# A long convolution and a switch layer on one core: the convolution in another stated order, its last round through the PSUM banks by halves

## The chip, the cores and the metric

The kernel runs on one core of a Trainium2 chip, written with Bass and Tile. The metric is the device time of one execution in microseconds. Before the change it is 543.25 us (median of three executions, 541.98 to 543.84). All rows below come from one further execution, recorded by the hardware profiler.

## The reference

A layer of an H3 model with 2048 tokens of 512 channels, followed by a mixture of 8 experts of which each token takes one.

```python
h  = x + q' * (conv(kv) + kv * ssm_D)        # q' = layernorm(x); x is A_q
#   kv = (4-tap causal convolution of A_k with shift_k) * A_v
#   conv(kv): causal convolution over all 2048 tokens with ssm_k,
#             channel by channel, in the reference by an FFT of length 4096
hn = layernorm(h)
e  = argmax(hn @ w_gate)                     # one expert per token
out = h + silu(hn @ w1[e]) @ w2[e]           # the gate of a single expert is 1
```

The means and variances of both layer norms go over the 512 channels of a token. All is in fp32.

## The kernel before

The program has three parts that follow one another: the convolution stage, in which `h` and the router's logits are made (until about 182 us), the routing (until about 196 us), and the experts (until the end). The change is in the first part; in the other two only a few small tables get another place in memory, and their instructions keep their order.

**The convolution stage.** The 512 channels are worked through in four blocks of 128 (`c` = 0 to 3), the 2048 tokens in four units of 512 (`u` = 0 to 3). The long convolution is a transform in two steps with a product between. For a block, the kernel does this, and each line names the engine:

- `first_tap` and `tap` (ScalarE, `L255`, `L263`), `add_tap` (GpSimd, `L267`) and, for the first block, `taps` (VectorE, `L272`) make the short convolution of A_k from the buffer `kt`, of which there is one. `turn_kv` (TensorE, `L279`) transposes it, `times_v` (VectorE, `L282`) multiplies by A_v.
- `stage_a` (TensorE, `L295`) is the transform's first step, once for the signal (`u`) and once for the channel's kernel (`k`), 16 times a block, through two PSUM buffers `pa`; `keep_a` (ScalarE, `L298`) brings each to SBUF.
- Then the block is taken in two halves of its channels, so that there are eight **rounds** `i` = 0 to 7. A round is a chain: `turn` for `u` and for `k` (VectorE, `L320`, 32x32 transposes into `xa` and `xb`); `stage_b("u")` (TensorE, `L331`, 16 matmuls of 32x32x512 over four banks of PSUM, the buffer `pb`); `keep_u` (ScalarE, `L337`, the four banks to SBUF); `stage_b("k1")`; `product1` (VectorE, `L340`); `stage_b("k2")`; `product2` (VectorE, `L344`); `back` (TensorE, `L331`, 32 matmuls: the way back); `unturn` (VectorE, `L352`).
- `pb` is one buffer of four banks. Each of the steps `stage_b`, `stage_b`, `stage_b`, `back` writes all of it anew, and so waits until the step before has been read.
- `last_stage` (TensorE, `L367`, through `pa`), `gate` (VectorE, `L371`), `residual` (GpSimd `L374`, on VectorE in the last block), `store_h`, `stats` (VectorE, `L381`, for the second layer norm), `turn_kv` of `h`, `keep_h` (ScalarE, `L384`), `logits` (TensorE, `L402`) and `sum_logits` (VectorE, `L411`) finish a block, unit by unit. `stats1` (VectorE, `L419`, `L420`) and `norm_x` (GpSimd, `L360`) are the first layer norm. `aggr` (VectorE, `L415`) closes the second. `stay_warm` (`L394`) issues matmuls without use at the end of the stage.

While a round's chain waits for another engine, an engine does the next block's first steps or the last block's last ones. The routing starts with `L646` (TensorE) and `L651` (VectorE), after the last `sum_logits` and `aggr`.

**What sets the order.** The steps are not written in the order of their issue. Each `add(...)` gives a step with its engine, an estimated cost, a due time, what it uses and what it makes; `Plan.run` then goes through them greedily and issues, engine by engine, the step that can start first and is due first. The tile framework sees the order of issue and puts the semaphores in. Every buffer (`BUF`, `PBUF`) is a ring of so many places; a place that is used again waits for the readers of what it held. Loads go through SyncE (SP) in the order of issue, and a load waits for the one eight places before it in its queue.

Of the kernel before, what the change touches and what calls it, by code (L numbers as in the profile page):

```python
# [11 lines left out]
I32 = mybir.dt.int32  # L12
# [19 lines left out]
for _n, _w in (("id", 128), ("b", 128), ("m", 128), ("tri", 128), ("one", 128),  # L32
               ("iota", 128), ("tile", 24), ("e", 8), ("key", 8), ("ta", 1), ("tb", 16),
               ("si", 64), ("ei", 64), ("cap", 8), ("tight", 64), ("ft", 128), ("scan", 128)):
    COLS[_n] = (C_N, C_N + _w)
    C_N += _w


class Plan:
# [33 lines left out]
    def run(self, pace, zero, ahead, latency=0.08, load=2.5, slack=0.25):  # L73
        ring = {b: [] for b in self.bufs}
        done, free, n_left = {}, {}, len(self.steps)
        need = [len(s[5]) for s in self.steps]
        then = [[] for _ in self.steps]
        for n, s in enumerate(self.steps):
            for m in s[5]:
                then[m].append(n)  # L80
        ready = {n for n, k in enumerate(need) if not k}
        moved = 0.0

        def start(n):
            eng, cost, due, fn, args, after, turn = self.steps[n]
            t = max(free.get(eng, 0.0), zero + pace * (due - ahead))
            wait = set(after)
            for b, k, place in turn:
                if place is not None and place != len(ring[b]):
                    return None  # L90
                if len(ring[b]) >= self.bufs[b]:
                    old = ring[b][-self.bufs[b]]
                    wait |= set(self.writers[old]) | set(self.readers[old])
            for m in wait:
                if m not in done:
                    return None
                e = self.steps[m][0]
                t = max(t, done[m] + (0.0 if e == eng else load if e == "SP" else latency))
            return t

        while n_left:
            best = {}
            for n in ready:
                t = start(n)
                if t is not None:
                    best.setdefault(self.steps[n][0], []).append((t, self.steps[n][2], n))
            assert best, [self.steps[n][3:5] for n in sorted(ready)[:9]]
            picks = []
            for c in best.values():
# [1113 lines left out]
```

## Time and profile before

| | us |
|---|---|
| median of three executions (541.98 to 543.84) | 543.25 |
| the profiled execution: its own time | 543.93 |
| the profiled execution: span from first to last instruction | 542.0 |
| convolution stage, to the first routing step of VectorE | 182.21 |
| the last round, from its first `stage_b` to the first `last_stage` behind it | 15.70 |
| from there to the first routing step of VectorE | 13.32 |

The profiled execution's time exceeds its span by 1.9 us and the median by 0.68 us. A row of a timeline has the start, the duration, the engine, the line, the operation with the tiles written and read, and the number of instructions that it groups; in square brackets stands how long the engine had been idle before, and which instruction of another engine ended that. The table of stretches shows which engine is full in a stretch: a busy time close to the stretch's length.

### The profile page before, as it was taken

How to read it: one execution, taken by the hardware profiler on the slowest of the kernel's cores; microseconds unless marked ns; L12 is line 12 of the kernel's file. 1: busy time of each engine (PE TensorE's matmuls, PEld its weight loads, DVE VectorE, ACT ScalarE, POOL GpSimd, SP SyncE). 2: the span in 40 equal slices, each digit the busy share in tenths (PEclk: the TensorE clock that was granted, in tenths of full speed). 3: DMA queues.
4: the chain of work that ended last, by engine and by line, in shares of the span. 5: the costliest groups of instructions: out<-in, count | busy, mean ns of one | idle time of the engine just before them, and what ended most of it. 6: DMA issues, size and time to landing. Idle time of an engine off the chain costs nothing.

```text
span 542.0 us, 12326 instructions
## 1 busy us (share of the span) xinstructions
PE 521.0 (96%) x4875; PEld 455.3 (84%) x4875; DVE 391.8 (72%) x556; ACT 264.6 (49%) x410; POOL 279.1 (52%) x324
## 2 busy tenths in 40 slices
PE   8999989999998989999999999999999999999994
PEld 8967777767656879689999999999988988988973
DVE  3779899898997979679655775864856765765851
ACT  2787887534321346545435444555544644554520
POOL 0455649865653237828703841850870850851832
PEclk9999999999999999999999999999999999999998
DMA  8919686659651378675554565665658557666401
GB/s 280 393 47 282 224 276 187 191 144 303 182 159 52 95 241 302 199 271 179 172 195 145 194 186 186 202 207 183 200 171 285 182 174 264 199 189 232 155 2 39
DMA packets 41156, 105.26 MB, mean 194 GB/s; under 512 B 5174, under 2 KB 13496, under 8 KB 40706
## 3 DMA queue, kind: packets, MB, share of 16 engines
q1 hardware_dynamic: 37682, 95.89, 53.9%
q0 software_dynamic: 3408, 8.51, 4.8%
q8 instruction: 40, 0.66, 0.5%
q14 instruction: 26, 0.21, 0.1%
HBM read 95.96 MB, written 8.50 MB: 193 GB/s over the span
## 4 chain that ended last, share of the span: by engine, by line
PE 80%; DVE 6%; issue 4%; DMA 4%; ACT 3%; POOL 1%; SPq 1%; POOLq 0%; DVEq 0%
PE acc L900 30%; PE acc L921 15%; PE acc L924 12%; PE pa L295 8%; PE pb L331 7%; PE pa L367 5%; DMA kt<-in_kt_dram 3%; PE pm L279 2%; PE pt L855 1%; DVE xa L344 1%; DVE zs L352 1%; DMA kt<-h_dram,idx 1%; PE pt L944 1%; DVE bst L381 1%; ACT ac L263 1%
## 5 line engine op out<-in xcount | busy, mean ns | idle before, releaser
L882 DVE TENSOR_TENSOR wlo<-raw,whi 128x1024 fp32r<-128x1024 f32 (+1 forms) x113 | 155.4, 1385 | 36.3 <-ACT whi L877 36.1
L905 POOL TENSOR_TENSOR hl<-s,hh 128x240 fp32r<-128x240 f32 (+5 forms) x112 | 102.8, 935 | 135.9 <-DVE hh L904 135.3
L877 ACT ACTIVATE whi<-raw 128x1024 fp32r<-128x1024 f32 x112 | 114.6, 1052 | 7.4 <-DMA raw<-in_w_dram 3.1
L903 ACT ACTIVATE s<-acc 128x240 f32<-128x240 f32 (+5 forms) x112 | 43.1, 387 | 113.0 <-PE acc L900 62.2
L904 DVE CAST hh<-s 128x240 fp32r<-128x240 f32 (+5 forms) x112 | 47.3, 430 | 54.4 <-ACT s L903 54.2
L900 PE MATMUL acc<-xh,whi 128*128 128x240 f32 (+5 forms) x448 | 72.6, 285 | 0.2 <-ACT xh L856 0.2
L900 PE MATMUL acc<-xl,whi 128*128 128x240 f32 (+5 forms) x448 | 71.8, 283 | 0.0
L900 PE MATMUL acc<-xh,wlo 128*128 128x240 f32 (+5 forms) x448 | 71.8, 283 | 0.0
L900 PEld LDWEIGHTS acc<-xh,whi 128*128 128x128 f32 x448 | 61.6, 189 | 0.9 <-ACT xh L856 0.4
L900 PEld LDWEIGHTS acc<-xl,whi 128*128 128x128 f32 x448 | 61.4, 189 | 0.0
L900 PEld LDWEIGHTS acc<-xh,wlo 128*128 128x128 f32 x448 | 61.3, 189 | 0.0
L921 PE MATMUL acc<-whi,hh 128*128 128x512 f32 (+2 forms) x136 | 54.4, 400 | 0.0
L921 PE MATMUL acc<-whi,hl 128*128 128x512 f32 (+2 forms) x136 | 53.7, 395 | 0.0
L921 PE MATMUL acc<-wlo,hh 128*128 128x512 f32 (+2 forms) x136 | 53.4, 393 | 0.0
L267 POOL TENSOR_TENSOR acc<-acc,ac 128x512 f32<-128x512 f32 x26 | 33.1, 1282 | 36.7 <-ACT acc L255 18.3
L924 PE MATMUL acc<-hh,whi 128*128 128x304 f32 (+2 forms) x168 | 49.7, 296 | 0.0
L924 PE MATMUL acc<-hl,whi 128*128 128x304 f32 (+2 forms) x168 | 49.2, 293 | 0.0
L924 PE MATMUL acc<-hh,wlo 128*128 128x304 f32 (+2 forms) x168 | 49.2, 293 | 0.0
L298 ACT ACTIVATE st<-pa 128x512 f32<-128x512 f32 x64 | 37.3, 595 | 19.6 <-PE pa L295 19.2
L295 PEld LDWEIGHTS pa<-kv,tw 128*128 128x128 f32 x256 | 30.2, 191 | 12.2 <-ACT st L298 8.7
L295 PE MATMUL pa<-kv,tw 128*128 128x128 f32 x256 | 33.5, 282 | 2.2 <-ACT st L298 2.2
L924 PEld LDWEIGHTS acc<-hh,whi 128*128 128x128 f32 x168 | 31.6, 188 | 0.1
(196 smaller groups left out, 892.4 us busy)
## 6 DMA issues: line engine op xcount, KB each, us to landing
raw<-in_w_dram SPq DMA_DIRECT2D x112, 512.0 KB, 4.2
tv<-in_tab_v_dram SPq DMA_DIRECT2D x12, 512.0 KB, 4.3
h<-in_q_dram SPq DMA_DIRECT2D x16, 256.0 KB, 5.1
kt<-in_kt_dram SPq DMA_DIRECT2D x3, 1216.0 KB, 8.0
v<-in_v_dram SPq DMA_DIRECT2D x12, 256.0 KB, 4.4
kern<-in_ssm_dram SPq DMA_DIRECT2D x12, 256.0 KB, 3.7
h<-in_x_dram SPq DMA_DIRECT2D x12, 256.0 KB, 3.5
h_dram<-h SPq DMA_DIRECT2D x12, 256.0 KB, 4.1
```

The lines of the kernel that those rows point to most:

```text
L267: nc.gpsimd.tensor_add(T[a, c, u], T[a, c, u], T[b, c, u])
L295: nc.tensor.matmul(p[:, :, j], tw[:, u * UJ + j, r, :], src[:, j, :], start=True, stop=True)
L298: nc.scalar.activation(T["s" + kind, c][:, r * NU + u], T["pa", kind, c, u, r], AF.Copy)
L331: nc.tensor.matmul(out[b, g, :], w[a], x[a, g, :], start=n == 0, stop=n == len(parts) - 1)
L877: nc.scalar.activation(whi, RAW[s], AF.Copy)
L882: nc.vector.tensor_sub(wlo[:, a:b], RAW[s][:, a:b], whi[:, a:b].bitcast(F32))
L900: nc.tensor.matmul(pu, a[:, k, at], b[:, k, :], start=i == k == 0, stop=i == 2 and k == ND - 1)
L903: nc.scalar.activation(s, pu, AF.Silu)
L904: nc.vector.tensor_copy(hh[:, f, :], s)
L905: nc.gpsimd.tensor_sub(hl[:, f, :], s, hh[:, f, :].bitcast(F32))
L921: nc.tensor.matmul(pd[:ds_.stop - ds_.start], b[:, f, ds_], a[:, f % 2, :], start=f == 0 and i == 0, stop=f == last - 1 and i == 2)
L924: nc.tensor.matmul(pd, a[:, f % 2, ds_], b[:, f, :], start=f == 0 and i == 0, stop=f == 2 * NCH - 1 and i == 2)
```

## The change

There are four parts.

1. **The order.** `Plan.run` with its costs, due times and pace is gone. A list `STEPS` names the 611 steps (603 before) in the order of their issue, and `run` only asserts that the list is possible. The set of steps is the same but for round 7; the order differs on all five engines throughout the convolution stage.
2. **The last round by halves.** For `i` = 7, `stage_b`, `keep_u`, `product1`, `product2`, `back` and `unturn` come twice, for the columns 0 to 255 and 256 to 511 of each of the four banks. The buffer `pb` is taken once for the whole round (`(buf, "both")`), and its halves are slices of it; `p1` likewise. `stay_warm` uses the same tile.
3. **Buffers.** `h` (rows of x) has four places instead of three, `ht` (the turned rows) three instead of two. The space comes from the constants: `cs` holds 1017 columns instead of 1281 (the load of its larger part is 128x889 instead of 128x1153), and the tables that the routing writes late (`mr0`, `tabs_e` and others) lie in a pool `latep` in the space that the convolution stage has left.
4. **The first loads.** `kt` for the first unit is the first DMA of SyncE (before, a table `tw` of 512 KB came first); the larger part of `cs` is the 15th (before, the 10th).

The core of the diff:

```diff
-    def run(self, pace, zero, ahead, latency=0.08, load=2.5, slack=0.25):
...
+    def run(self, order):
+        assert sorted(order) == list(range(len(self.steps)))
+        ring, made = {b: [] for b in self.bufs}, set()
+        for n in order:
             eng, cost, due, fn, args, after, turn = self.steps[n]
...
-               h=(3, quad), xn=(2, quad), tv=(2, [P, UJ, 2, P]), ht=(2, quad))
+               h=(4, quad), xn=(2, quad), tv=(2, [P, UJ, 2, P]), ht=(3, quad))
...
+    def four(buf, key):
+        make = pt if buf == "pb" else sb
+        if len(key) == 2:
+            return make(buf, key, *([[P, NG, 512]] if buf == "pb" else []))
+        if not taken[buf]:
+            make(buf, (buf, "both"), *([[P, NG, 512]] if buf == "pb" else []))
+        half = len(taken[buf]) % 2
+        taken[buf].append(key)
+        T[key] = T[buf, "both"][:, :, 256 * half:256 * half + 256]
+        return T[key]
...
-    def stage_b(kind, k, i):
-        blocks(pt("pb", ("b" + kind, i), [P, NG, 512]), [(k, by_group(T["t" + kind[0], i]))], False)
+    def stage_b(kind, k, i, *y):
+        blocks(four("pb", ("b" + kind, i, *y)), [(k, by_group(T["t" + kind[0], i], *y))], False)
...
+            for y in range(2):
+                tu, tk = [("tu", i), ("tu", i, y)], [("tk", i)]
+                add("PE", 0.7, 0, stage_b, "u", 0, i, y, uses=[*tu, "cb"], behind=["pb"] if y else [],
+                    makes=([] if y else [("pb", "pb")]) + [("pb2", ("bu", i, y))])
+                add("ACT", 1.0, 0, keep_u, i, y, uses=[("bu", i, y), ("tu", i)], mods=[("tu", i, y)])
+                add("PE", 0.7, 0, stage_b, "k1", 1, i, y, uses=[*tk, "cb"], behind=[("bu", i, y)],
+                    makes=[("pb2", ("bk1", i, y))])
...
+                add("PE", 1.25, 0, back, i, y, uses=[("p1", i, y), *tu, "cb"], makes=[("pb2", ("pz", i, y))])
+                add("DVE", 1.2, 0, unturn, i, y, uses=[("pz", i, y)], puts=[("zs", c)])
...
+    STEPS = """
+    48 1 52 49 0 50 54 74 75 2 55 51 6 76 77 56 53 59 57 80 66 60 82 7 81 65 78 84 83 58 68 91 63 8 79 61 62 85 70
...
-    plan.run(PACE, ZERO, AHEAD)
+    plan.run([int(n) for n in STEPS.split()])
```

What the order of the built program shows at the three places that matter most. In these rows `[waits ...]` names the engines or DMA queues whose semaphores an instruction waits on.

TensorE in the last round, before: the logits of an earlier unit, `stage_b("k2")` for round 7, one `last_stage`, `back`.

```order
L402 MATMUL pm<-ht,wgc 32x128 [waits Activation_49]
L402 MATMUL pm<-ht,wgc 32x128 x7
L331 MATMUL pb<-xa,cb 32x512 [waits DVE_49]
L331 MATMUL pb<-xa,cb 32x512 x15
L367 MATMUL pa<-zs,tv 128x128 [waits DMAHW2_49]
L367 MATMUL pa<-zs,tv 128x128 x7
L331 MATMUL pb<-p_2090,cb 32x512 [waits DVE_49]
L331 MATMUL pb<-p_2090,cb 32x512 x15
L331 MATMUL pb<-xb,cb 32x512 x16
```

TensorE at the same place now: `stage_b("k2")` for the first half, one `last_stage` (`pa<-zs,tv`), `stage_b("k2")` for the second half, `back` for the first and for the second half.

```order
L306 MATMUL pb<-xa,cb 32x256 [waits DVE_49]
L306 MATMUL pb<-xa,cb 32x256 x15
L346 MATMUL pa<-zs,tv 128x128 [waits DMAHW5_49]
L346 MATMUL pa<-zs,tv 128x128 x7
L306 MATMUL pb<-xa,cb 32x256 [waits DVE_49]
L306 MATMUL pb<-xa,cb 32x256 x15
L306 MATMUL pb<-p_2112,cb 32x256 [waits DVE_49]
L306 MATMUL pb<-p_2112,cb 32x256 x15
L306 MATMUL pb<-xb,cb 32x256 x16
L306 MATMUL pb<-p_2112,cb 32x256 [waits DVE_49]
L306 MATMUL pb<-p_2112,cb 32x256 x15
L306 MATMUL pb<-xb,cb 32x256 x16
```

The single steps have become pairs, and each of the five groups begins with a wait for VectorE; the `last_stage` stands between the two halves of `stage_b("k2")`.

VectorE in the last round, before: `product1`, two groups of `stats` with one `sum_logits` between, `product2`, one `gate`, `unturn`, one `sum_logits`.

```order
L340 TENSOR_TENSOR p_2090<-pb,xb 128x2048 [waits PE_49,Activation_49]
L381 BN_STATS bst_64<-h 128x6 [waits Pool_49]
L381 BN_STATS bst_64<-h 128x6 x3
L411 TENSOR_TENSOR lacc<-pm,lacc 128x128 [waits DVE_49,PE_49]
L381 BN_STATS bst_64<-h 128x6 [waits Pool_49]
L381 BN_STATS bst_64<-h 128x6 x3
L344 TENSOR_TENSOR xb<-pb,xb 128x2048 [waits DVE_49,PE_49]
L371 TENSOR_TENSOR xn<-pa,xn 128x512 [waits PE_49,Pool_49]
L352 STREAM_TRANSPOSE zs<-pb 128x64x16x2 [waits PE_49]
L411 TENSOR_TENSOR lacc<-pm,lacc 128x128 [waits DVE_49,PE_49]
```

VectorE there now: the halves of `product1`, a `sum_logits`, the halves of `product2` with a `gate` between, the halves of `unturn`, then `stats`.

```order
L315 TENSOR_TENSOR p_2112<-pb,xb 128x4x256 [waits DVE_49,PE_49,Activation_49]
L315 TENSOR_TENSOR p_2112<-pb,xb 128x4x256 [waits PE_49]
L388 TENSOR_TENSOR lacc<-pm,lacc 128x128 [waits DVE_49]
L319 TENSOR_TENSOR xb<-pb,xb 128x1024 [waits DVE_49,PE_49]
L350 TENSOR_TENSOR xn<-pa,xn 128x512 [waits Pool_49]
L319 TENSOR_TENSOR xb<-pb,xb 128x1024 [waits DVE_49,PE_49]
L331 STREAM_TRANSPOSE zs<-pb 128x32x16x2 [waits PE_49]
L331 STREAM_TRANSPOSE zs<-pb 128x32x16x2
L360 BN_STATS bst_64<-h 128x6 [waits Pool_49]
L360 BN_STATS bst_64<-h 128x6 x7
L350 TENSOR_TENSOR st<-pa,st 128x512 [waits PE_49]
L360 BN_STATS bst_64<-h 128x6 x4
```

The `stats` groups that stood behind the products stand behind `unturn` now. The second half of `product1`, like the first, waits for TensorE, and the second half of `unturn` has no wait of its own.

VectorE before round 2, before: `turn("u", 2)`, three `stats1` (each a BN_STATS and a BN_AGGR), two `times_v`, `turn("k", 2)`.

```order
L320 STREAM_TRANSPOSE xa<-st 128x2048 [waits Activation_49]
L419 BN_STATS bst_100<-h 128x6 [waits DMAHW3_49,DVE_49]
L420 BN_AGGR mva<-bst_100 128x2 [waits DVE_49]
L419 BN_STATS bst_100<-h 128x6 [waits DMAHW4_49]
L420 BN_AGGR mva<-bst_100 128x2 [waits DVE_49]
L419 BN_STATS bst_100<-h 128x6 [waits DMAHW2_49,DVE_49]
L420 BN_AGGR mva<-bst_100 128x2 [waits DVE_49]
L282 TENSOR_TENSOR kv<-pm,v 128x512 [waits PE_49]
L282 TENSOR_TENSOR kv<-pm,v 128x512 [waits DMAHW0_49,PE_49]
L320 STREAM_TRANSPOSE xb<-st 128x2048
```

VectorE there now: `turn("u", 2)`, one `times_v`, `turn("k", 2)`, a `stats1`.

```order
L295 STREAM_TRANSPOSE xa<-st 128x2048 [waits Activation_49]
L242 TENSOR_TENSOR kv<-pm,v 128x512 [waits DMAHW3_49,PE_49]
L295 STREAM_TRANSPOSE xb<-st 128x2048
L396 BN_STATS bst_100<-h 128x6 [waits DMAHW1_49]
L397 BN_AGGR mva<-bst_100 128x2 [waits DVE_49]
```

The three `stats1` and one `times_v` have gone from between the two turns.

## Rows read from the trace of the kernel before

**Rows 1.** The page's first part: the span, and TensorE's busy time with its share and instructions.
```profile
span 542.0 us, 12326 instructions
...
PE 521.0 (96%) x4875; PEld 455.3 (84%) x4875; DVE 391.8 (72%) x556; ACT 264.6 (49%) x410; POOL 279.1 (52%) x324
```

**Rows 2.** The table of stretches. The edges are the starts of the eight rounds' first `stage_b` (28.95, 46.00, 66.49, 87.33, 104.15, 120.59, 137.24, 153.19), the start of the first `last_stage` behind the last round (168.89) and the first routing step of VectorE (182.21). The columns: the stretch, its length, the busy time of each engine with its instructions, TensorE's granted clock (1.00 is full speed), the DMA engines' share, GB/s.
```profile
7.45:28.95 21.50, 20.64 (x169) 19.76 (x168) 15.43 (x28) 12.98 (x22) 6.54 (x15) 1.00 0.91 353
28.95:46.00 17.05, 16.07 (x246) 11.16 (x245) 14.80 (x14) 15.20 (x24) 11.82 (x10) 1.00 0.39 102
46.00:66.49 20.49, 19.81 (x277) 14.90 (x276) 18.55 (x25) 15.82 (x26) 11.33 (x10) 1.00 0.79 267
66.49:87.33 20.84, 19.21 (x273) 14.44 (x272) 19.59 (x27) 16.27 (x25) 13.32 (x16) 1.00 0.75 237
87.33:104.15 16.82, 16.79 (x265) 11.96 (x264) 14.75 (x17) 10.02 (x15) 15.37 (x21) 1.00 0.60 186
104.15:120.59 16.44, 16.33 (x261) 11.55 (x260) 15.14 (x18) 8.66 (x13) 12.38 (x15) 1.00 0.63 177
120.59:137.24 16.65, 16.65 (x254) 12.11 (x253) 14.77 (x17) 7.14 (x10) 8.25 (x17) 1.00 0.82 264
137.24:153.19 15.95, 14.54 (x253) 9.19 (x253) 15.18 (x19) 3.67 (x4) 9.25 (x16) 1.00 0.64 189
153.19:168.89 15.70, 13.02 (x237) 7.27 (x237) 13.28 (x21) 3.67 (x4) 9.87 (x14) 1.00 0.36 102
168.89:182.21 13.32, 12.86 (x126) 11.48 (x127) 11.86 (x48) 2.39 (x4) 0.00 (x0) 1.00 0.28 81
```

**Rows 3.** The timeline of TensorE in the last round (`pb`) and behind it. A matmul of fp32 stands as two in the profile, so that 16 matmuls read x32. In turn: `stage_b("u")`, one `last_stage`, `stage_b("k1")`, `stage_b("k2")`, one `last_stage`, the first half of `back`, and the first two `last_stage` of the last block.
```profile
153.19 1.15 PE L331 MATMUL pb<-xb,cb 32*32 32x512 f32 x32 [0.40 <-DVE zs L352]
154.27 2.08 PE L367 MATMUL pa<-zs,tv 128*128 128x128 f32 x16
156.45 1.15 PE L331 MATMUL pb<-xa,cb 32*32 32x512 f32 x32
...
160.19 1.15 PE L331 MATMUL pb<-xa,cb 32*32 32x512 f32 x32 [0.29 <-DVE p L340]
161.28 2.08 PE L367 MATMUL pa<-zs,tv 128*128 128x128 f32 x16
164.13 1.15 PE L331 MATMUL pb<-p,cb 32*32 32x512 f32 x32 [0.78 <-DVE xb L344]
...
168.89 3.90 PE L367 MATMUL pa<-zs,st 128*128 128x128 f32 x32 [0.65 <-DVE zs L352]
```

**Rows 4.** The timeline of VectorE in the same stretch: `stats`, `product1`, `stats`, `stats`, `product2`, `unturn`, `stats`, `gate`.
```profile
155.84 0.83 DVE L381 BATCH_NORM_STATS2 bst<-h 128x6 f32<-128x128 f32 x4
...
157.85 2.29 DVE L340 TENSOR_TENSOR p<-pb,xb 128x2048 f32<-128x2048 f32 x1 [0.58 <-PE pb L331]
160.05 0.86 DVE L381 BATCH_NORM_STATS2 bst<-h 128x6 f32<-128x128 f32 x4
...
161.02 0.86 DVE L381 BATCH_NORM_STATS2 bst<-h 128x6 f32<-128x128 f32 x4
161.80 2.27 DVE L344 TENSOR_TENSOR xb<-pb,xb 128x2048 f32<-128x2048 f32 x1
...
166.52 2.32 DVE L352 STREAM_TRANSPOSE zs<-pb 128x2048 f32<-128x2048 f32 x1 [1.84 <-PE pb L331]
...
168.93 0.85 DVE L381 BATCH_NORM_STATS2 bst<-h 128x6 f32<-128x128 f32 x4
171.01 0.69 DVE L371 TENSOR_TENSOR st<-pa,st 128x512 f32<-128x512 f32 x1 [1.22 <-PE pa L367]
```

**Rows 5.** The timeline of ScalarE in the same stretch: `keep_u`.
```profile
154.51 1.88 ACT L337 ACTIVATE xb<-pb 128x2048 f32<-128x2048 f32 x1 [6.08 <-PE pb L331]
```

**Rows 6.** The page's group of `keep_a` (a copy of 512 elements from PSUM): busy time, mean ns of one, idle before, releaser.
```profile
L298 ACT ACTIVATE st<-pa 128x512 f32<-128x512 f32 x64 | 37.3, 595 | 19.6 <-PE pa L295 19.2
```

**Rows 7.** The timeline of TensorE in rounds 0 to 2: what follows `back(0)` (two `stage_a`, two `turn_kv`, one `stage_a`), and, in round 2, three `stage_a` and `stage_b("k1")`.
```profile
42.25 2.05 PE L295 MATMUL pa<-kv,tw 128*128 128x128 f32 x16
44.14 1.04 PE L279 MATMUL pm<-cs,acc 128*128 128x128 f32 x8
45.01 1.06 PE L295 MATMUL pa<-kern,tw 128*128 128x128 f32 x8
...
70.24 3.00 PE L295 MATMUL pa<-kv,tw 128*128 128x128 f32 x24 [1.52 <-ACT st L298]
73.17 1.14 PE L331 MATMUL pb<-xb,cb 32*32 32x512 f32 x32
```

**Rows 8.** The timeline of VectorE between the two turns of round 2: `turn("u")`, a `times_v` of round 1 (57.10), two `times_v`, `turn("k")`.
```profile
57.10 0.68 DVE L282 TENSOR_TENSOR kv<-pm,v 128x512 f32<-128x512 f32 x1
...
63.59 2.31 DVE L320 STREAM_TRANSPOSE xa<-st 128x2048 f32<-128x2048 f32 x1 [0.50 <-ACT st L298]
...
68.34 1.25 DVE L282 TENSOR_TENSOR kv<-pm,v 128x512 f32<-128x512 f32 x2
69.52 2.30 DVE L320 STREAM_TRANSPOSE xb<-st 128x2048 f32<-128x2048 f32 x1
```

**Rows 9.** The timeline of ScalarE at the start: the first `first_tap`.
```profile
6.69 0.72 ACT L255 ACTIVATE acc<-kt,shw_sb 128x512 f32<-128x512 f32 x1 [4.46 <-DMA kt<-in_kt_dram]
```

**Rows 10.** The page's DMA issues: `store_h`; KB each, median us from issue to landing.
```profile
h_dram<-h SPq DMA_DIRECT2D x12, 256.0 KB, 4.1
```

More of the change, by code (lines that the diff above doesn't have):

```diff
@@ L94, in start @@
[L94 to L109, printed above, removed]
-                t0 = min(c)[0]
-                _, n, t = min((due, n, t) for t, due, n in c if t <= t0 + slack)
-                picks.append((t, n))
-            t, n = min(picks)
-            eng, cost, due, fn, args, after, turn = self.steps[n]
-            for b, k, place in turn:
+                    assert made.issuperset(self.writers[old]) and made.issuperset(self.readers[old])
@@ L116, in run @@
                 ring[b].append(k)
             fn(*args)
-            done[n] = free[eng] = t + cost
-            if eng == "SP":
-                free[eng] = t + 0.42
-                done[n] = moved = max(moved, free[eng]) + cost
-            ready.remove(n)
-            n_left -= 1
-            for m in then[n]:
-                need[m] -= 1
-                if not need[m]:
-                    ready.add(m)
-        return max(done.values())
+            made.add(n)
 @with_exitstack
@@ L143 @@
     h_rows = h_dram.rearrange("(p j) d -> p j d", j=NJ)
-    cs = keep.tile([P, C_N], F32, name="cs")
+    cs = keep.tile([P, C_K], F32, name="cs")
     def const(n):
@@ L390, in stay_warm @@
     def stay_warm(n):
-        if "late" not in T:
-            pt("pb", "late", [P, NG, 512])
         for _ in range(n):
-            nc.tensor.matmul(T["late"][:, 0, :P], const("one"), cs[:, :P], start=True, stop=True)
+            nc.tensor.matmul(T["pb", "both"][:, 0, :P], const("one"), cs[:, :P], start=True, stop=True)
     def logits(c, p):
@@ L572 @@
-            add("DVE", 2.3, t + DG[4], product1, i, uses=[("bk1", i), ("tu", i)], makes=[("p1", ("p1", i))])
-            add("PE", 1.2, t + DG[5], stage_b, "k2", 2, i, uses=[("tk", i), "cb", ("p1", i)],
-                makes=[("pb", ("bk2", i))])
-            add("DVE", 2.3, t + DG[6], product2, i, uses=[("bk2", i), ("p1", i)], mods=[("tu", i)])
-            add("PE", 2.25, t + DG[7], back, i, uses=[("p1", i), ("tu", i), "cb"], makes=[("pb", ("pz", i))])
-            add("DVE", 2.33, t + DG[8], unturn, i, uses=[("pz", i)],
-                **(dict(puts=[("zs", c)]) if i % NH else dict(makes=[("zs", ("zs", c))])))
+                    makes=[(turned(kind, i), ("t" + kind, i))] + [(None, ("tu", i, y)) for y in range(2) if kind == "u"])
```

128 lines of the change are left out of this document (71 added, 57 removed), and 21 rows, old and new, of the table STEPS.

## The prediction

> **What bounds the kernel now.** I read the page's first part first: TensorE is busy 521.0 of 542.0 us [rows 1]. That is an average over three parts with different limits, and the change is in the first of them. So the next view is the table of stretches, cut at the first `stage_b` of each round [rows 2]. What to see there is how much of each stretch TensorE leaves idle, since no order of the same steps can take out more than that. In rounds 3, 4 and 5 it is 0.03, 0.11 and 0.00 us: they are full. In rounds 0, 1 and 2 it is 0.98, 0.68 and 1.63 us, in round 6 1.41, in the last round 2.68. The granted clock is 1.00 in all of them, so nothing is to be had from the clock.
>
> The last round and what follows are of another kind. There I read the timelines of TensorE, VectorE and ScalarE side by side [rows 3 to 5]. The round is one chain over the four banks: start of `stage_b("u")` to `keep_u` 1.32, `keep_u` 1.88, a handoff of 0.06, `k1` to `product1` 1.40, `product1` 2.29, 0.05, `k2` to `product2` 1.61, `product2` 2.27, 0.06, `back` to `unturn` 2.39, `unturn` 2.32, 0.05: together 15.70, the length of the stretch. No engine is full; VectorE fills its waits with three groups of `stats` (155.84, 160.05, 161.02). In the 13.32 us behind it VectorE has 11.86 us of work [rows 2] and one idle place of 1.22 us, before 171.01 [rows 4]; there VectorE is what counts.
>
> **Part 1, the order until the last round.** At the start, `first_tap` waits 4.46 us for `kt` [rows 9], behind a table of 512 KB. At the 353 GB/s of that stretch 512 KB are 1.5 us, an estimate; TensorE was idle for only 0.86 us of 7.45 to 28.95 [rows 2]. The gain lies between 0 (the larger constants, now 15th, come late to VectorE's `small_parts`) and 2.4 (both added). I take 0.85 us: with a pipeline that was 96% full, an earlier beginning is not all kept.
>
> Round 0: behind `back(0)` stand two `stage_a`, two `turn_kv` and one `stage_a`, 3.75 us until the next `stage_b("u")` [rows 2, 7]. Now it is two `stage_a` and the sum of the router's weights, 1.0 us less, and 0.1 for an idle gap: 1.1 us shorter. Round 1 gets the moved steps and two further `stage_a` (about 1.0 each [rows 7]), less the sum of weights: 1.35 us longer. Round 2: `turn("k", 2)` starts at 69.52, 3.62 us after `turn("u", 2)` has ended (63.59 + 2.31) [rows 8]; `stage_b("k1")` starts 6.68 us behind `stage_b("u")` (73.17 less 66.49), with three `stage_a` that were late by 1.52 us [rows 2, 7]. Now one `times_v` (0.68) stands between the turns, and TensorE has one `turn_kv` (0.52, half of 1.04) and two `stage_a` (2.0) behind 1.14 us of `stage_b`: 3.7 us. So `k1` comes 3.0 us earlier within the round; one `turn_kv` less behind it gives 0.4 more: 3.4 us. The three together are 3.15 us. The order allows a test of this sum: TensorE has done the same 73 steps before `stage_b("u", 3)` in both programs, so the three rounds can't lose more than their idle time of 3.29 us. The sum is near that bound; below, nothing at all may be gained.
>
> Rounds 3 to 5 are full and do the same steps: 0. Round 6 takes one more `last_stage`, 2.08 us [rows 3], which stood in the last round: 14.54 + 2.08 = 16.62 against 15.95, so 0.67 us longer. The lead at the last round is 0.85 + 3.15 - 0.67 = 3.33 us.
>
> The buffers of `h` and `ht` I cost at 0: what hides their loads is a DMA share of 0.39 to 0.79 in rounds 0 to 2 [rows 2], and TensorE, not a load, is full after that. The late tables wait for the last stores of `h`, which land 4.1 us after their issue [rows 10]; the first of these tables is written some twenty VectorE steps into the routing, so 0; without that cover, up to 4.1 us.
>
> **Part 2, the last round by halves.** The halves are columns of the same four banks. In VectorE's order the second half of `product1` waits for TensorE again, though its data were there with the first: it waits for `k2` of the first half. `unturn` of the first half waits, that of the second doesn't: both halves of `back` are waited for. I take `keep_u` to wait for both halves of `stage_b("u")` in the same way. So a step on one half waits for the other engine's step on the other half, and the two engines take turns over the banks. The work is cut in two and nothing runs beside anything. The prices of halves are not in the trace. A product is 2.29 us for 2048 elements and 0.68 for 512 [rows 4, 8]; half lies between, on the straight line at 1.22. `keep_u`: 1.88 and 0.595 give 1.02 [rows 5, 6]. `unturn` has no smaller row; its half lies between 0.68, the short product, and 2.32; I take 1.2, as for the product. A half `stage_b` takes 0.57 of TensorE, and 0.78 until VectorE starts; half of `back` 1.25 (between half and all of 2.39). The chain then: 1.35 to `keep_u`, 2.05 for both of its halves, 0.06, `k1` 1.40, `product1` 1.22 + 0.05, then the half of `k2` and the `last_stage` that stands before the other half, 0.57 + 2.08, during which `product1`'s second half is done, the other half of `k2` 0.78, `product2` 1.28, `back` 1.25, `product2` 1.28, `back` 1.25, both halves of `unturn` 2.45. The sum is 17.0 us against 15.70: 1.3 longer. With halves at exactly half it would be about 16.0; with the four half products at 2.29, 21.3. I take 17.0, and 16.0 to 18.5 as likely.
>
> The rows of the order show only that the waits are there. The Trainium skill, PSUM — Partial Sum Buffer, section "PSUM bank collisions raise a hardware error", says why: two engines may not touch the same bank in the same 32 partitions at one time, even in disjoint columns, and PSUM is to be guarded by bank and not by address. By that rule the last round is the 17.0 us above; without it, the 10.1 us of the first rival. No row before shows two engines in one bank, so the trace of before neither bears it out nor speaks against it.
>
> **Part 3, behind the last round.** Three groups of `stats` that lay in the last round's waits now stand behind `unturn`. Each takes 0.78 us (the distance from 160.05 to the next step at 160.83; the row has 0.86 with its end) [rows 4], 2.34 together. Two of the four groups there fill TensorE's first `last_stage`, and the idle 1.22 us shrinks by 0.65. The rest is 1.7 us, on VectorE, which is what counts there. Bounds: 1.1, if all of the 1.22 is filled, and 2.4, if none.
>
> **The sum.** -3.33 + 1.3 + 1.7 = -0.3 us. Against the profiled execution's 543.93 that is 543.6; that execution was 0.68 us above the median, so that 542.9 answers to the median. I predict 543.2. What a measurement of this kernel can tell from no change is about 0.3%, 1.6 us: the band is 541.6 to 544.9.
>
> **Rivals.**
> A, the halves do overlap, wholly or in part. Then VectorE runs the four half products without a break: 0.78 + 1.02 + 0.06 + 0.78 + 4 x 1.22 + 0.06 + 1.25 + 1.2 + 0.05 = 10.1 us, 5.6 less than before, and the sum is 543.93 - 3.33 - 5.6 + 1.7 = 536.7; with half of that overlap 540. For it: VectorE is idle before `unturn` for 1.84 us and TensorE for 2.68 in that round [rows 2, 4], time that halves could use. Against it: the waits in the order.
>
> B, slower: the lead isn't made, because what held TensorE in rounds 0 to 2 is ScalarE. `stage_a` has two buffers and waits for `keep_a`; the 1.52 us before 70.24 ended with ScalarE's copy [rows 7], and ScalarE is busy 15.20 of 17.05, 15.82 of 20.49 and 16.27 of 20.84 us [rows 2]. It works in order, and a tap that waits for `kt` or for GpSimd holds each `keep_a` behind it. Then the 3.15 us fall away and the end keeps its price: 543.93 - 0.85 + 0.67 + 3.0 = 546.75. It decides as soon as the lead at the last round is below 1.4 us (3.0 less 1.6). Against it: in rounds 3 to 5 ScalarE has 10 us and less, and there TensorE was full with the same two buffers.
>
> C, the order changes little in the early rounds and the end is cheap, because the alternation costs only its handoffs (16.0) and the idle place takes the `stats` (1.1): 543.93 - 0.18 + 0.3 + 1.1 = 545.15 with no lead but the start's; with the lead, 542.0. Both ends lie about the band's edges, so this is counted as the forecast's own spread.
>
> **How the numbers follow.** A 0.17, the forecast with its spread 0.58, B 0.25. The forecast's own range is 541.0 to 545.5: of its 0.58, 0.15 are faster than the band, 0.38 in it, 0.05 slower. Of B 0.02 fall into the band. So faster 0.32, same 0.40, slower 0.28. The range for 8 of 10 reaches up to B's 546.8 and down to 539.0, which leaves out most of A and little of B.
>
> **What would show it.** The start of `stage_b("u", 3)` at 83.3 (87.33 before) and of the last round at 149.9 shows part 1 right; 86 or later there, with TensorE idle for ScalarE, is B. In the last round the rows on `pb` must alternate between the engines, with 17 us from the first `stage_b` to the first `last_stage` behind it, and a `last_stage` between the halves of `k2` that holds VectorE; `product1`'s second half beside TensorE's `k2` in time, or a length near 10 us, is A. Behind it the first routing step of VectorE should come 15.0 us after that `last_stage`, with `stats` in the gap before the first `gate`. The experts should take the same time to 0.5 us; if they don't, the sum rests on the wrong part of the kernel.

## The result: slower, and of two kinds

The changed kernel takes 548.07 us (median of seven executions, 545.44 to 549.00), the kernel before 543.62 in the same comparison: 1.0076 times as long, 95% interval 1.0055 to 1.0098. That is outside the range, and on the slower side. The executions are of two kinds, which the median hides: three of the seven are at 545.4 to 546.4 us, four at 548.1 to 549.0. The mean granted clock is 0.992 to 0.996 in the first and 0.982 to 0.985 in the second. The profiled execution (546.02 us, span 544.1) is of the first kind, so what follows first is the account of 2.1 us; the second kind has its own trace further down.

The table of stretches of the changed kernel, cut at the same events as [rows 2]:

```profile
29.36:45.52 16.16, 15.72 (x242) 10.70 (x241) 14.54 (x13) 14.38 (x22) 11.73 (x10) 1.00 0.50 149
45.52:67.21 21.69, 21.69 (x298) 17.05 (x297) 20.68 (x31) 18.20 (x30) 14.05 (x12) 1.00 0.67 217
67.21:85.03 17.82, 17.20 (x258) 12.55 (x257) 17.26 (x22) 10.62 (x16) 8.44 (x13) 1.00 0.68 227
85.03:101.82 16.79, 16.79 (x265) 11.96 (x264) 14.49 (x17) 10.12 (x15) 11.84 (x15) 1.00 0.69 217
101.82:118.57 16.75, 16.75 (x265) 11.96 (x264) 15.73 (x19) 11.04 (x17) 14.10 (x20) 1.00 0.70 216
118.57:135.01 16.44, 16.25 (x250) 11.67 (x249) 14.84 (x17) 6.60 (x10) 8.47 (x12) 1.00 0.53 164
135.01:151.54 16.53, 16.23 (x270) 11.05 (x269) 15.41 (x19) 4.27 (x5) 10.61 (x17) 1.00 0.73 225
151.54:169.56 18.02, 11.54 (x365) 7.27 (x365) 10.60 (x12) 3.51 (x5) 11.89 (x21) 1.00 0.33 104
169.56:184.94 15.38, 15.01 (x153) 13.25 (x153) 13.96 (x60) 2.28 (x4) 0.00 (x0) 1.00 0.36 103
```

Put beside [rows 2], length by length: the first `stage_b` starts 0.41 us later (29.36 for 28.95). Rounds 0, 1 and 2 are 16.16, 21.69 and 17.82 us (17.05, 20.49, 20.84): together 2.71 shorter. Rounds 3 to 5 together are the same to 0.07 (singly -0.03, +0.31 and -0.21), round 6 is 0.58 longer. So the last round starts 1.65 us earlier, at 151.54. Then 18.02 us for 15.70, and 15.38 for 13.32. The first routing step comes at 184.94 for 182.21, 2.73 late; routing and experts give 0.63 back (359.16 for 359.79 to the span's end), a little more than the 0.5 that the prediction allowed, which leaves 2.1.

`k1` of round 2, to be set against 73.17 in [rows 7]:

```profile
70.65 1.14 PE L306 MATMUL pb<-xb,cb 32*32 32x512 f32 x32
```

TensorE in the last round (the rows that answer to [rows 3]; the first column is the start in us, the second the duration, the bracket the idle time before and what ended it):

```profile
151.54 1.50 PE L306 MATMUL pb<-xb,cb 32*32 32x256 f32 x64
...
155.06 1.49 PE L306 MATMUL pb<-xa,cb 32*32 32x256 f32 x64 [1.44 <-ACT xb L312]
...
157.93 0.73 PE L306 MATMUL pb<-xa,cb 32*32 32x256 f32 x32 [0.80 <-DVE p L315]
158.59 2.08 PE L346 MATMUL pa<-zs,tv 128*128 128x128 f32 x16
160.60 0.71 PE L306 MATMUL pb<-xa,cb 32*32 32x256 f32 x32
162.78 0.73 PE L306 MATMUL pb<-p,cb 32*32 32x256 f32 x32 [1.47 <-DVE xb L319]
...
165.59 0.73 PE L306 MATMUL pb<-p,cb 32*32 32x256 f32 x32 [1.32 <-DVE xb L319]
...
169.56 3.89 PE L346 MATMUL pa<-zs,st 128*128 128x128 f32 x32 [1.45 <-DVE zs L331]
```

VectorE there ([rows 4]):

```profile
156.65 1.23 DVE L315 TENSOR_TENSOR p<-pb,xb 128x1024 f32<-128x1024 f32 x1 [2.64 <-issue]
158.83 1.23 DVE L315 TENSOR_TENSOR p<-pb,xb 128x1024 f32<-128x1024 f32 x1 [0.96 <-PE pb L306]
...
161.50 1.22 DVE L319 TENSOR_TENSOR xb<-pb,xb 128x1024 f32<-128x1024 f32 x1 [1.24 <-PE pb L306]
...
164.31 1.23 DVE L319 TENSOR_TENSOR xb<-pb,xb 128x1024 f32<-128x1024 f32 x1 [0.99 <-PE pb L306]
167.12 2.38 DVE L331 STREAM_TRANSPOSE zs<-pb 128x1024 f32<-128x1024 f32 x2 [1.59 <-PE pb L306]
```

To be seen: the steps on `pb` never overlap. `product1`'s first half ends at 157.88, `k2`'s first half starts at 157.93; VectorE's second half waits until 158.83 though its own data were there; each half of `back` waits for one half of `product2` and the other way round. From the first half of `product1` on both engines stand idle in turn, 0.8 to 1.6 us each time. The 2.08 us of a `last_stage` between the halves of `k2` lie on the same chain: VectorE's `product2` waits behind it.

### The profile page after: what moved, and what is told of

The parts are those of the page before. It is cut to its first block, busy times and chain, and to the rows that moved or that the text cites. A ratio compares the mean times of both kernels' runs of the same rounds, so it can differ in the third digit from the quotient of the medians.

```text
span 544.1 us, 12641 instructions
## 1 busy us (share of the span) xinstructions
PE 522.8 (96%) x5035; PEld 457.6 (84%) x5035; DVE 390.1 (72%) x559; ACT 262.9 (48%) x411; POOL 275.4 (51%) x324
## 4 chain that ended last, share of the span: by engine, by line
PE 72%; DVE 11%; issue 6%; DMA 5%; POOL 2%; ACT 2%; SPq 0%; POOLq 0%; DVEq 0%; ACTq 0%
PE acc L921 26%; PE acc L942 13%; PE acc L945 12%; PE pb L306 6%; PE pa L346 5%; PE pa L255 5%; PE pm L239 1%; PE pt L876 1%; DVE bst L396 1%; DMA raw<-in_w_dram 1%; DVE p L315 1%; DMA zs<-in_ssm_dram 1%; POOL hl L926 1%; DVE acc L232 1%; DVE xb L319 1%
```

## The experiments

Theory H: the halves are the loss, because the two engines take turns over one buffer. Theory O: the order is the loss. All edits are against the changed kernel unless said otherwise, and are cut to their core (`...` marks a cut; where steps are moved, the steps are given by name). Each kernel was timed beside the kernel before on the same chip, and the ratios are to that.

**e1, the last round whole.** Each pair of halves is one step again, at the first half's place.

```diff
-            if i < NH * ND - 1:
+            if i < NH * ND:
```

> The changed kernel, but the last round whole again (its order otherwise untouched). Theory H (the halves are the loss: the engines take turns over the banks, 18.02 us against 15.70, and TensorE, with 2.5 of 4 us busy from 152 to 172, is granted a lower clock a little later): the last round takes 15.5 to 16.0 us, the granted clock stays at 1.00 from 192 to 200 us, the time is 2 to 4 us below the changed kernel's, 543.5 to 545. Theory O (the order is the loss: a start that is 0.4 us later and three groups of stats moved behind the last round): the last round shortens but the time stays above 546.

543.54 us, ratio 1.0004 (0.9990 to 1.0017). The last round takes 16.42 us (15.5 to 16.0 expected), part of it at a low clock (0.50 from about 160 to 163 us), the stretch behind it still 15.38. The `last_stage` behind `k2`, 2.08 us at the full clock:

```profile
159.60 3.52 PE L346 MATMUL pa<-zs,tv 128*128 128x128 f32 x16
```

Theory H: without the halves the kernel is back at the kernel before's time. This doesn't mean that the order is neutral: the early lead (1.67 us at the last round) is there, and the longer last round and the stretch behind it use it up; e12 shows the lead by itself. The expectation of 1.00 from 192 to 200 us missed: the clock also falls between 188 and 198 us in every trace here but the kernel before's and e7's. With that fall the later parts of the changed kernel were no longer than the kernel before's (359.16 for 359.79 us).

**e2, the kernel before's order with the changed kernel's buffers.**

```diff
-            if i < NH * ND - 1:
+            if i < NH * ND:
...
-    48 1 52 49 0 50 54 74 75 2 55 51 6 76 77 56 53 59 57 80 66 60 82 7 81 65 78 84 83 58 68 91 63 8 79 61 62 85 70
+    6 1 48 0 52 74 2 54 59 3 63 7 84 49 50 75 51 55 76 53 8 56 80 60 182 81 77 66 61 82 67 214 57 78 83 65 58
```

> The kernel before's order of steps and whole last round, with the changed kernel's buffers (four of h, three of ht), constants and late tables. Both theories: the buffers cost and bring nothing, 542.5 to 544.5, the rounds' starts within 0.3 us of the kernel before. If it is 546 or more, the buffers or the tables' place are the cause, and both theories fall.

543.39 us, 0.9997 (0.9985 to 1.0009). The buffers, the shorter constants and the late tables cost and bring nothing. One part of the expectation missed: the first `stage_b` starts at 29.46 us, 0.51 behind the kernel before's, not within 0.3; by round 2 the difference is 0.10 (66.59).

**e3, the halves in the old order.** As e2, with the last round's steps cut in two in place (the first of the changed lines, by the steps' names):

```diff
-PE stage_b(u,7)  ACT keep_u(7)  PE stage_b(k1,7)  DVE product1(7)
+PE stage_b(u,7,0) stage_b(u,7,1)  ACT keep_u(7,0) keep_u(7,1)  PE stage_b(k1,7,0) stage_b(k1,7,1)  DVE product1(7,0) product1(7,1)
```

> As the run before, but with the last round by halves (each step's two halves one behind the other). Theory H: the last round 17 to 18 us, the granted clock falls behind it, 545.5 to 548. Theory O: 543.5 to 544.5, since the order of before is kept.

545.13 us, 1.0030 (1.0018 to 1.0043). The last round takes 16.77 us, 1.07 more than [rows 3], the stretch behind it 13.33. So the halves cost in the old order too, but only half as much, and both numbers are a little below the expectation (17 to 18 us, 545.5 to 548). There the two halves of `k2` stand side by side, without a `last_stage` between, and VectorE's `stats` lie in the waits; that this is what makes the 1.07 of the 2.32 us is argued from the orders, and was not run by itself.

**e4, the halves in two tiles of two banks.**

```diff
+                four_banks.close()
+                two = four_banks.enter_context(tc.tile_pool(name="two", bufs=1, space=PSUM))
+                T[buf, 0], T[buf, 1] = (two.tile([P, 2, 512], F32, name=f"half{y}") for y in range(2))
+        half = key[-1]
...
-        T[key] = T[buf, "both"][:, :, 256 * half:256 * half + 256]
+        T[key] = T[buf, half]
```

A half is then 32 channels in two banks with all 512 columns; its 8 matmuls take 1.09 us where 16 short ones took 0.73. So the half steps themselves are not cheaper on TensorE than in the changed kernel.

> The changed kernel's order, the halves cut by banks: two tiles of two banks each, so that no step on one half waits for a step on the other. A half stage_b uses 8 of the 16 tiles of 32x32. If it is the turn-taking over one tile that costs (theory H in its narrow form), the last round takes 12.5 to 14 us, and the time is 4 to 6 us below the changed kernel's: 541.5 to 544. If halving itself costs (more instructions, short matmuls), the last round stays at 16 us or more and the time at 545 or more.

541.09 us, 0.9957 (0.9941 to 0.9972): faster than both kernels. VectorE and TensorE in its last round:

```profile
155.34 2.36 DVE L323 TENSOR_TENSOR p<-half,xb 128x1024 f32<-128x1024 f32 x2 [1.11 <-PE half L314]
...
157.81 1.23 DVE L327 TENSOR_TENSOR xb<-half,xb 128x1024 f32<-128x1024 f32 x1
...
160.85 1.23 DVE L327 TENSOR_TENSOR xb<-half,xb 128x1024 f32<-128x1024 f32 x1 [0.33 <-PE half L314]
162.53 1.25 DVE L339 STREAM_TRANSPOSE zs<-half 128x1024 f32<-128x1024 f32 x1 [0.46 <-PE half L314]
164.18 1.25 DVE L339 STREAM_TRANSPOSE zs<-half 128x1024 f32<-128x1024 f32 x1 [0.40 <-PE half L314]
```

```profile
151.75 1.14 PE L314 MATMUL half<-xb,cb 32*32 32x512 f32 x32
...
156.62 1.09 PE L314 MATMUL half<-xa,cb 32*32 32x512 f32 x16
...
162.13 1.09 PE L314 MATMUL half<-p,cb 32*32 32x512 f32 x16
...
165.49 3.90 PE L354 MATMUL pa<-zs,st 128*128 128x128 f32 x32 [0.39 <-DVE zs L339]
```

The two halves of `product1` run as one piece from 155.34 to 157.70, and `k2`'s first half starts at 156.62 beneath the second. `product2` follows without a wait at 157.81. The round is 13.74 us (151.75 to 165.49). So it is the turn-taking that costs, not the halving. e4 gives each half a tile of its own and banks of its own at once; whether two halves of one tile would overlap if they lay in different banks was not run, so the runs don't tell whether the waits are there for the tile or for the bank. This agrees with the Trainium skill's rule (PSUM — Partial Sum Buffer, "PSUM bank collisions raise a hardware error") as far as it says that different banks may be used at once; that columns of one bank may not was not tried.

**e5, the changed kernel again; e13, e14, e15, three further traces of it.**

> The changed kernel once more, to see its executions beside the kernel before's on one chip, and another trace. Of its seven executions so far four were 548 to 549 us at a mean granted clock of 0.982 to 0.985, three 545.4 to 546.4 at 0.992 to 0.996; the profiled one is of the second kind. If the slower kind belongs to this kernel (theory C: the idle TensorE of the last round brings a second, longer stretch at the low clock), more than half of the executions are at 547.5 or above, and a trace of one shows where the clock is low. If it was the chip of that day, all are at 545 to 546.5 and the clock is 0.988 or more, as the kernel before's.

546.34 us, 1.0063 (1.0037 to 1.0088); four executions at 545.6 to 546.3, three at 548.0 to 548.5. Neither expectation came as said: the slower kind is there, but in three of seven and not in more than half. (What the expectation calls the second kind, the profiled one, is the faster, here the first.) One of the three, at 548.01, has a mean clock of 0.991, so that its loss isn't to be seen in that number. The trace is again one of the first kind.

> The changed kernel unchanged, for a trace of one of its executions at 548 us (7 of 14 so far), of which none is traced. Theory C: in such an execution the granted clock is at 0.5 for some microseconds within the last round (152 to 170 us), as in the traces of e1, e11 and e12, and the last round takes 19.5 to 21 us instead of 18.0; the rest is as in the traces at 546. If the last round is 18.0 us there too, the two microseconds lie in the experts, and theory C falls.

(e14 and e15 were expected to be the same as e13, each with about one chance in two of being at 548 us.) 548.38, 545.84 and 549.32 us, beside 543.50 for the kernel before: e13 and e15 are of the second kind. The stretches of e13, and then of the changed kernel's first trace; TensorE's granted clock is the last number but two:

```profile
151.19:164.00 12.81, 9.02 (x293) 5.60 (x292) 6.98 (x9) 2.43 (x3) 7.02 (x14) 1.00 0.47 148
164.00:176.00 12.00, 10.18 (x104) 8.52 (x104) 7.18 (x18) 1.20 (x2) 4.91 (x8) 0.57 0.01 1
176.00:187.71 11.71, 11.34 (x124) 9.57 (x122) 10.40 (x45) 2.28 (x4) 0.00 (x0) 1.00 0.47 136
```

```profile
151.54:164.00 12.46, 8.75 (x293) 5.60 (x292) 6.94 (x8) 2.43 (x3) 6.63 (x14) 1.00 0.47 149
164.00:176.00 12.00, 9.23 (x157) 7.79 (x139) 9.26 (x23) 1.08 (x2) 5.26 (x8) 1.00 0.11 32
176.00:184.94 8.94, 8.57 (x90) 7.13 (x88) 8.37 (x40) 2.28 (x4) 0.00 (x0) 1.00 0.47 136
```

In e13 the clock goes to its lower level (0.5, 1.2 of 2.4 GHz) at about 164.7, while TensorE waits for the second half of `product2`, and comes back at about 175; the mean of 164 to 176 is 0.57. Before it fell, TensorE had been busy for 9.02 of 12.81 us in short pieces; in the first trace it had been busy for 8.75 of 12.46 us, and the clock didn't fall. The pair of `last_stage` that begins behind `unturn` shows the price:

```profile
165.24 1.17 PE L306 MATMUL pb<-p,cb 32*32 32x256 f32 x32 [1.32 <-DVE xb L319]
166.09 1.52 PE L306 MATMUL pb<-xb,cb 32*32 32x256 f32 x32
...
170.09 6.13 PE L346 MATMUL pa<-zs,st 128*128 128x128 f32 x32 [0.58 <-DVE zs L331]
```

6.13 us for what took 3.89 (169.56 above). The last round is 18.90 us (19.5 to 21 expected), the stretch behind it 17.62 (15.38). So the low clock of theory C is there, but its place was off: most of the loss lies behind the last round, not in it. e15 has the same, with a low clock from about 164.7 to 175 us; e14 has 1.00 there.

**e6, useless matmuls in TensorE's waits.**

```diff
+    def fill(m, n):
+        pf = pt("pm", ("fill", m), [P, P])
+        for _ in range(n):
+            nc.tensor.matmul(pf, const("one"), cs[:, :P], start=True, stop=True)
...
+    for m, n in enumerate((4, 2, 4, 4, 4)):
+        add("PE", 0.2 * n, 0, fill, m, n, uses=["cs"], makes=[("pm", ("fill", m))])
```

> The changed kernel with 18 matmuls of 128x128 without use put into TensorE's five waits of the last round (4 before k1, 2 before k2, 4 before each half of back, 4 before the first last_stage), into the PSUM buffer pm; nothing waits for them. Theory C: the granted clock is 0.988 or more in nearly all executions and the time 545 to 546.5, 1.5 to 2.5 us below the changed kernel's beside it. If the idle time of TensorE in the last round is not what lowers the clock: the same clocks and times as the changed kernel beside it, or up to 0.5 us more.

545.86 us, 1.0044 (1.0029 to 1.0059); twelve executions at 545.1 to 546.8, none of the second kind, the clock 0.989 to 0.993. In the trace TensorE is busy 12.05 of 13.02 us before 164:

```profile
150.98:164.00 13.02, 12.05 (x316) 8.42 (x316) 7.19 (x9) 2.43 (x3) 7.54 (x14) 1.00 0.49 147
164.00:176.00 12.00, 11.46 (x159) 9.93 (x158) 9.49 (x24) 1.09 (x2) 4.72 (x8) 1.00 0.16 45
```

In the same comparison it was three of seven executions of the second kind without the fill (e5) and none of twelve with it; over all runs of the changed kernel it was nine of seventeen. That speaks for the idle TensorE of the last round as what makes the low clock likely; the counts are small, and how idle it must be is not shown. The traces agree: the clock fell within the last round in e13 and e15, and in e1, e11 and e12, whose last rounds are whole (e1: TensorE busy for 4.84 of the 8.38 us before the fall), and in none where TensorE has more to do in that round (13.02 of 15.70 us in e2, 12.76 of 13.74 in e4). Against the first kind the fill gains nothing: the last round is 18.02 us as before (150.98 to 169.00), and the turn-taking stays. Beside e5's median it is 0.5 us faster, not the 1.5 to 2.5 expected, since that median was of the first kind.

**e7, e4 with three groups of stats back in the last round.**

```diff
 DVE gate(2,2)
+DVE stats(2,0)
 DVE product1(7,0)  product1(7,1)  sum_logits(2,0)  product2(7,0)
+DVE stats(2,1)
 DVE gate(2,3)  product2(7,1)
+DVE stats(2,2)
 DVE unturn(7,0)  unturn(7,1)  stats(2,3)
-DVE stats(2,2)
```

(`stats(2,1)` and `stats(2,0)` leave their later places too.)

> The two-tile kernel (e4) with three groups of stats taken from behind the last round back into VectorE's waits in it: one before product1, one behind each half of product2. If the stats behind the last round are on the path at their full price (2.34 us less 0.65 of idle time, 1.7), the stretch from the first last_stage of the last block to the routing falls from 15.4 to 13.6 to 14.0 us, the last round grows by at most 0.4, and the time is 539.3 to 540.2. If TensorE's work sets that stretch, it stays at 15 us and the time at 540.5 to 541.5.

541.19 us, 0.9953 (0.9938 to 0.9968), the same as e4. The stretch behind the last round is 15.37 us as before. VectorE has 11.82 us of work in it instead of e4's 13.96. So in this order the moved `stats` were not on the path.

**e9, e7 with the old order behind the last round.** On all engines the steps after `back` stand as in the kernel before; VectorE's from `unturn` on:

```diff
-stats(2,3) gate(3,0) residual(3,0) gate(3,1) residual(3,1) gate(3,2) stats(3,0) sum_logits(2,1) residual(3,2) gate(3,3)
-residual(3,3) aggr(0) sum_logits(3,0) stats(3,2) stats(3,3) sum_logits(3,1) stats(3,1) aggr(3) aggr(1) aggr(2)
+sum_logits(2,1) stats(2,3) gate(3,0) residual(3,0) stats(3,0) gate(3,1) residual(3,1) aggr(0) gate(3,2) residual(3,2)
+stats(3,1) gate(3,3) residual(3,3) sum_logits(3,0) aggr(1) stats(3,2) aggr(2) stats(3,3) sum_logits(3,1) aggr(3)
```

> Run e7 (two tiles, the stats in the last round), with the steps behind back in the kernel before's order on all engines. Theory T (what made the end longer is not the moved stats but what stands behind the last sum_logits on VectorE: one stats and three aggr, 2.5 us, where the kernel before has one aggr, 0.8; and TensorE's logits(2,1) and turn_kv in another order): the stretch from the first last_stage of the last block to the routing is 13.3 to 13.7 us (15.37 in e7), the time 538.8 to 539.8. If TensorE's or ScalarE's pace sets the stretch whatever VectorE's order is, it stays above 14.8 and the time at 540.5 or more.

539.56 us, 0.9921 (0.9905 to 0.9936), the fastest of all. The stretch is 13.32 us, as in [rows 2]. The last round is 14.50 us (13.74 in e7), because a `logits` lies in it now, so the two together are 1.29 us shorter. VectorE at the stretch's end in e7, then in e9 (`sum_logits` is `lacc<-pm,lacc`, then what stands before the routing's `mx`):

```profile
178.13 0.29 DVE L396 TENSOR_TENSOR lacc<-pm,lacc 128x128 f32<-128x128 f32 x1 [0.39 <-PE pm L387]
178.34 0.86 DVE L368 BATCH_NORM_STATS2 bst<-st 128x6 f32<-128x128 f32 x4
179.11 1.59 DVE L400 BATCH_NORM_AGGREGATE rec<-bst 128x2 f32<-128x24 f32 x12
180.62 0.23 DVE L674 TENSOR_REDUCE mx<-pl 128x16 f32<-128x128 f32 x1
```

```profile
178.01 0.27 DVE L396 TENSOR_TENSOR lacc<-pm,lacc 128x128 f32<-128x128 f32 x1
178.20 0.62 DVE L400 BATCH_NORM_AGGREGATE rec<-bst 128x2 f32<-128x24 f32 x4
178.84 0.29 DVE L674 TENSOR_REDUCE mx<-pl 128x16 f32<-128x128 f32 x1
```

In the stated order one `stats` and three `aggr` (12 instructions) stand behind the last `sum_logits`, which waits for TensorE: 2.49 us from there to the routing. In the old order one `aggr` stands there: 0.83. That is 1.66 of the 2.05 us; the other 0.4 is the last `sum_logits` itself, 12.88 and 12.49 us behind the stretch's start, in the stated order behind a `logits(2,1)` among the `last_stage`. e9 has e7's `stats` in the last round too; the old end with these `stats` behind the round was not run. It could not have been 13.32 us, as VectorE has 13.96 us of work there in e4.

**e8 and e10, the start.** e8 is e4 with a shorter warm-up, e10 is e9 with that and another order of the first DMAs.

```diff
-    for _ in range(30):
+    for _ in range(20):
```

In e10, SP's first DMAs:

```diff
-kt(0:7) shw v(0:2) dsk kt(7:11) ssm(0:1) id tw kt(11:19)
+kt(0:7) shw id tw v(0:2) dsk kt(7:11) ssm(0:1) kt(11:19)
```

> The two-tile kernel (e4) with 20 instead of 30 matmuls of 128x128 before the first transposes. In the changed kernel the taps of the first unit are done at 7.4 us (9.7 before), but TensorE's warm-up ends at 11.1. If it is the warm-up that ate the earlier kt, the first turn_kv starts near 7.6 to 8 us and the first stage_b 0.8 to 2 us earlier (27.6 to 28.8 against 29.56), and the time falls with it to 539.5 to 540.5, unless the clock falls early. If the tables tw or ScalarE set the start, the first stage_b stays at 29.3 to 29.7.

540.77 us, 0.9951 (0.9936 to 0.9966), no clear gain over e4; the first `stage_b` at 29.10, between the two expectations. TensorE's start:

```profile
9.37 0.63 PE L241 MATMUL pm<-cs,acc 128*128 128x128 f32 x4 [0.34 <-DMA cs<-in_cst_dram]
11.40 1.13 PE L257 MATMUL pa<-zs,tw 128*128 128x128 f32 x8 [1.40 <-DMA tw<-in_tab_w_dram]
```

The first `stage_a` waits for the table `tw`, which the change had put behind `kt`. Part of what the earlier `kt` gave is so paid back with a later `tw`.

> Run e9 with 20 warm-up matmuls and the first DMAs in another order: kt's first part, shw, the identity, the table tw, and then the rest as in the changed kernel. In e8 TensorE waited 0.34 us for the identity and 1.40 us for that table after a shorter warm-up. If these two waits are the start's delay, the first stage_b comes at 27.3 to 28.4 us instead of 29.1 to 29.6 and the time is 0.7 to 1.5 us below e9. If VectorE's taps or ScalarE set the start, it stays within 0.4 us of e9.

542.35 us, 0.9968 (0.9954 to 0.9981), 2.8 us worse than e9: a miss. The first `stage_b` starts at 33.21. The identity and `tw` ahead of the rest make `zs` late (VectorE waited 5.11 us for it, until 12.56), TensorE did nothing from 10 to 12 us, and the granted clock was 0.50 from 14 to 20.

**e11 and e12, the stated order without halves, with the old end.** e11 is e1 with the old order of all engines from `stage_b("u", 7)` on, e12 is e9 with each pair of halves one step in one buffer. Beside the changed order of the steps, the edit of both is

```diff
-            if i < NH * ND - 1:
+            if i < NH * ND:
```

> Run e1 (the changed kernel's order, the last round whole) with the kernel before's order from the last round's first stage_b on. It is the stated order up to the last round alone. By theory T the lead of 1.65 us at the last round comes through: last round 15.6 to 16.0, the stretch behind it 13.3 to 13.6, the time 541.3 to 542.3 (before: 543.3 to 543.6). If the early lead is bought with work put off, as the prediction's slower rival had it for TensorE, the time is 543 or more.

545.31 us, 1.0022 (1.0009 to 1.0035), a miss, spoiled by the mixing of two orders: the last round is 20.01 us, the stretch behind it 13.32. GpSimd did three `norm_x` (5.16 us) before the residual for which TensorE's next transposes wait, `k2` stood behind them and came at 162.22, and the clock was at 0.50 from about 156 to 164.

> Run e9 with the last round whole again (one buffer of four banks), the stats in its waits and the kernel before's order behind it; it puts right what spoiled e11, where GpSimd did three norm_x before the residual that TensorE's next transposes wait for. It is the stated order up to the last round, alone. If the lead of 1.65 us or more at the last round comes through: last round 15.6 to 16.2 us, the stretch behind it 13.3 to 13.6, the time 541.3 to 542.5, some 2 us above e9 and 1 to 2 us below the kernel before. If the lead is lost at the end: 543 or more.

541.71 us, 0.9968 (0.9953 to 0.9982). The lead of the early rounds comes through (last round from 151.38, then 13.33 us). The last round itself is 16.42 us, not the 15.6 to 16.2 expected, with 0.50 of clock from about 160 to 163. This kernel has no halves, so the low clock is not theirs alone.

## Why the prediction was wrong

The forecast was -0.3 us; the profiled execution has +2.1, and about every second one 2.2 more. Three steps failed: the gain at the start, the price of the half steps in the last round, and the clock, which was put at nothing. A fourth came out at nearly its size for the wrong reason. Step by step:

1. **The start, -0.85: failed.** Measured +0.41, and +0.04 to +0.48 over five traces of the changed kernel. That it is later at all is not shown, since the old order with the new buffers starts 0.51 later too (e2); the gain is not there. I took the wait of [rows 9] for the limit and asked only what is late if the constants come later. What was late next is the table that had stood ahead of `kt`: behind the shorter warm-up of e8 the first `stage_a` waits 1.40 us for it. Neither it nor the warm-up (until 11.1 us) was in the sum. The table and the identity ahead didn't help (e10): then the next load, `zs`, was late.
2. **Rounds 0 to 2, -3.15: right.** -2.71, and each with its sign and nearly its size: -0.89 (-1.1), +1.20 (+1.35), -3.02 (-3.4). `k1` of round 2 follows `stage_b("u")` by 3.44 us (3.7 worked out, 6.68 before). Rounds 3 to 5 and round 6 came as said (+0.07, +0.58 for 0 and 0.67). Rival B has the wrong place: ScalarE did not hold TensorE. That the first kind's 546 us lie near B's 546.75 is chance.
3. **The last round, +1.3: right in kind, too small.** The turn-taking is there as the order's waits said. Measured +2.32. The term that was mis-sized is the half step on TensorE: 16 matmuls of 256 columns take 0.73 us, not half of 1.15, so that VectorE starts 0.90 us after a half of `k2` (0.78 assumed) and 1.53 after each half of `back` (1.25), and ScalarE 1.53 and VectorE 1.59 after the pairs (1.35 and 1.40). Rival A fell; e4 shows how halves overlap, and even there the round is 13.74 us, not A's 10.1. The prediction gives the banks as the reason for the waits; the runs show only that the waits are gone with two tiles in different banks, and leave open whether the tiles or the banks do it.
4. **Behind the last round, +1.7: the size nearly, the reason wrong.** Measured +2.06. I charged three moved `stats` to VectorE; e7 took them away and nothing changed. What costs is the order behind the last `sum_logits` (e9: 1.66 us), and a `logits` that lies in this stretch and no longer in the last round (0.4). Both stood in the order of the program, and I did not price them. That the size came nearly right is luck.
5. **The clock: missing.** No step and no rival had it. I read "1.00 in all of them" in [rows 2] as "nothing is to be had from the clock", and did not ask what a last round with less work for TensorE (11.54 of 18.02 us, 13.02 of 15.70 before) puts at risk. It is 2.2 us in nine of seventeen executions, and moves the median out of the range; the executions of the first kind lie in it.

The buffers and late tables at 0 were right (e2). Over the profiled execution the sum failed by the start (1.26), the last round (1.02), rounds 0 to 2 (0.44), the end (0.36), less the 0.63 that the later parts gave back: 2.4 us, in an execution of the first kind.

## What to carry to other kernels

Cutting a step in two pays only if the halves don't share what they are guarded by: here column halves of one PSUM tile take turns, halves in two tiles of two banks each overlap, and against the kernel before, the new order included, this is 2.5 us faster (e4) instead of 3.1 to 4.5 slower (e5 and the result). Behind the last wait of a stage only what needs that wait should stand: one `aggr` instead of one `stats` and three `aggr`, 1.7 us. And a stage that leaves TensorE idle in pieces can be paid for a second time, where the clock falls: here in about every second execution.

## What was not expected of the hardware

Halving a matmul's columns saves a third of its duration, not half. The changed kernel's `L306`, from the view of one line (durations in ns: least, median, most; then the time of the first and the last, and the shapes):

```profile
L306 PE MATMUL pb<-p,cb x288: 374/587/612, 40.4 to 165.9; 32*32 32x512 f32 x112, 32*32 32x256 f32 x32
```

The least, 374 ns, is that of 256 columns; 587 is that of 512. What waits for the matmuls says the same: VectorE starts 0.90 us after a half of `k2`, and 1.61 after a whole one [rows 3, 4]. And the low clock is a matter of chance between executions of one program: of the changed kernel's seventeen, nine took 548 us or more; the two of these that were traced had 0.50 from about 165 to 175 us, the three traced others 1.00, with the same work. It stayed low for some 10 us (e13), the last 5 of them with TensorE full (from 170 on).
